# Local attention in 20 chunks of 116 or 112 queries instead of 24 of 96, with q and k of a chunk in one load

## The chip, the cores and the metric

The kernel runs on one core of a Trainium2 chip. The metric is the device time of one execution in microseconds (us). A core has a matrix engine (PE, with its weight loads shown apart as PEld), a vector engine (DVE), an activation engine (ACT), a general engine (POOL), and a queue engine (SP) that here only issues DMAs. Each engine works through its own instructions in the order in which the program issues them.

## What is computed

Three stages in float32. B, H, S, D are 4, 8, 576, 64, so there are 2304 tokens of 512 values.

```python
# local + downsampled attention (S = 576, factor = 4)
q_d, k_d, v_d = (x.reshape(B, H, S // 4, 4, D).mean(axis=3) for x in (q, k, v))
out_up = np.repeat(sm_attn(q_d, k_d, v_d), 4, axis=2)
mask = np.abs(pos[:, None] - pos[None, :]) < 4
scores = np.where(mask, scale * q @ k.T, -1e9)
attn = np.exp(scores - max); attn = attn / (sum + 1e-09)
x = (out_up + attn @ v).reshape(B * S, H * D)
# MoE1, then MoE2, 512 -> 2048 -> 512 on each token
h = x @ w_in;  x = (h * sigmoid(h)) @ w_out
h = x @ w_in2; out = (P(h) / (Q(h) + 1e-6)) @ w_out2
```

The weights and activations of the two MoE stages are each split into a high and a low part, and a product takes three matmuls (high by high, low by high, high by low).

## The kernel before, in words

**Attention** is made batch by batch (`attention(b)`, line 375). For each batch three loads bring k and q (line 392, 192 queries each). The downsampled attention takes sums of four (line 408 for batch 0, accumulating DMAs at lines 435 and 437 for the others) and runs through lines 471 to 526. The local attention of a batch is cut into 6 chunks of 96 queries, each two halves of 48 that lie on partitions 0 and 64. A chunk is a chain of jobs:

- S, lines 569 to 583, on PE: two matmuls of 216 columns that put the band mask into PSUM, and 16 small matmuls of 64 rows and 54 keys. The trace records each small float32 matmul twice, so S has 2 + 32 records.
- M (587), E (593 and 597, eight exponentials), U (602 and 603, sum and reciprocal), N (606, normalizing).
- T, line 617, on PE: eight transposes of 48 queries; C (line 627, the copy function at 332 or 328) brings them to SBUF.
- O, line 637, on PE: 16 small matmuls of 48 columns with v (32 records).
- A (644) adds the downsampled part, H (655) and X (659) split the result into `xh` and `xl`.

**MoE1** runs over 5 blocks of tokens: four of 5 chunks (480 columns) and one of 4 chunks (384 columns). A block takes 16 steps, one for each 128 rows of the hidden layer. A step has 12 matmuls at line 807 (h) and, two steps later, 12 at line 821 (o); all have as many columns as the block. Blocks 0 and 1 are interleaved: 8 steps of block 0, 16 of block 1, 8 of block 0, then blocks 2 to 4 (`PART1`, line 311). Step 0 needs all chunks of block 0, step 8 all of block 1.

**The weights** arrive as float64 and are converted on the chip, 64 pieces with seven jobs each on DVE, ACT and POOL (`piece`, line 699). MoE1's pieces must be ready for steps 0 to 7 (w_in, w_out of f = 0 to 7) and 16 more for steps 16 to 23. MoE2's are converted while MoE1 runs.

**The order of the work** on every engine until the end of MoE1 is set when the program is built: a planner (`Plan.run`, line 122) simulates the jobs with assumed costs, due times, and rings of buffers, and emits them in the order of its simulation. In the first part it also puts matmuls that compute nothing (line 289, 256 columns) where it expects PE to idle. MoE2 (from line 1041) follows in a written order, 5 blocks of 512 or 384 tokens.

Of the kernel before, what the change touches and what calls it, by code (L numbers as in the profile page):

```python
# [10 lines left out]
F32 = mybir.dt.float32  # L11
# [10 lines left out]
CH = 96  # L22
SUB = 48
HALO = 3
WK = SUB + 2 * HALO
TH = 2 * CH
KW = TH + 2 * HALO
QPAD = 16
BLOCKS1 = [5, 5, 5, 5, 4]
# [18 lines left out]
NKQ = 4  # L48
# [200 lines left out]
def r_ns(n, count):  # L249

    return count * (n / 2.4 + 14)
# [3 lines left out]
def tile_kernel(ctx, tc, kq, kqs, vp, vw_in, moe_w_in, moe_w_out, moe2_w_in, moe2_w_out, moe2_a, moe2_b, out):  # L255
# [10 lines left out]
    NCH = S // CH  # L266
    NB1 = max(BLOCKS1) * CH

# [36 lines left out]
    chunk_block = [(j, i) for j, n in enumerate(BLOCKS1) for i in range(n)]  # L305
    tok0, t = [], 0
    for n in BLOCKS1:
        tok0.append(t)
        t += n * CH

# [5 lines left out]
    for j, f in STEP1:  # L316
        guess.append(t)
        t += 24 * (BLOCKS1[j] * CH / 2.4 + 14) * PACE
# [23 lines left out]
    E_t = [at.tile([128, 8, 64], F32, tag=f"E{i}", name=f"E{i}", bufs=1) for i in range(NE)]  # L342
# [18 lines left out]
    nc.vector.memset(bands[64:128, 2, :, WK - HALO:WK], NEG)  # L361
    for e in E_t:
        nc.gpsimd.memset(e[:, :, WK:], 0.0)
        nc.gpsimd.memset(e[:, :, WK:WK + 1], 1e-9)
# [10 lines left out]
    def attention(b):  # L375
# [6 lines left out]
        def tail(b, c):  # L382
            j, i = chunk_block[b * NCH + c]
            return when[j * NF] - LEAD + 300.0 * i


        loads = []
        for t in range(3):
            u = kqu[t] = Unit("kq")
            def ld(e, t=t):  # L390
                kqt[t] = at.tile([128, KT * (KW + TH) + QPAD], F32, tag="kq", name="kq", bufs=NKQ)
                nc.sync.dma_start(out=kqt[t], in_=kq[b, t])
            loads.append(plan.add(f"L{b}{t}", FAR, {"D": 60}, ld, take=[u],
                                  size=128 * 4 * 1576))
# [3 lines left out]
        if b == 0:  # L398
            for t in range(3):
                for w in range(2):  # L400
                    def sm(e, t=t, w=w):
                        if w == 0:
                            o = kd[:, :, SUB * t:SUB * t + SUB]
                            i = kqt[t][:, :KT * KW].rearrange("p (g s) -> p g s", g=KT)[:, :, HALO:HALO + TH]
                        else:
                            o = qd[:, :KT * SD].rearrange("p (g s) -> p g s", g=KT)[:, :, SUB * t:SUB * t + SUB]
                            i = kqt[t][:, KT * KW:KT * (KW + TH)].rearrange("p (g s) -> p g s", g=KT)
                        nc.vector.tensor_reduce(out=o, in_=i.rearrange("p g (j r) -> p g j r", r=4), axis=AX.X, op=ALU.add)
                    sums.append(plan.add(f"R{b}{t}{w}", FAR, {"V": v_ns(768)}, sm, after=[loads[t]] + sums[:1],
                                         take=[] if sums else [kdu], give=[kqu[t]]))  # L410
# [49 lines left out]
        for m in range(2):  # L460
# [4 lines left out]
            def s(e, x=x, m=m, p0=p0):  # L465
                x["s"] = pair(p0)
                for t in range(3):
                    for a in range(2):
                        for e_ in range(2):
                            r, g = slice(64 * e_, 64 * e_ + 64), 2 * m + a  # L470
                            nc.tensor.matmul(x["s"][64 * a:64 * a + 64, e_, SD * t:SD * t + SD],  # L471
                                             lhsT=qd[r, SD * g + SUB * t:SD * g + SUB * t + 64], rhs=kd[r, g, :],
# [26 lines left out]
            def tr(e, x=x, e_=0, u=None):  # L499
                x["t", e_] = pair(u)  # L500
                for t in range(3):
                    for kk in range(2):
                        for a in range(2):
                            r = slice(64 * a, 64 * a + SUB)
                            nc.tensor.transpose(x["t", e_][:HS, a, SD * kk + SUB * t:SD * kk + SUB * t + SUB],
                                                x["e"][r, 3 * e_ + t, HS * kk:HS * kk + HS], ident[r, r])
# [39 lines left out]
        for c in range(NCH):  # L546
            x = {}
            j, i = chunk_block[b * NCH + c]
            due = begin[j] - (TAIL1 if j == 1 else TAIL) - (STAG if j else STAG0) * (BLOCKS1[j] - 1 - i)
            t, q0 = c // 2, CH * (c % 2)  # L550
# [18 lines left out]
            def s(e, x=x, c=c, t=t, q0=q0, pS=pS):  # L569
# [5 lines left out]
                for g in range(KT):  # L575
                    for s_ in range(2):
                        for e_ in range(2):
                            r = slice(64 * e_, 64 * e_ + 64)
                            k0 = KW * g + q0 + SUB * s_
                            l0 = KT * KW + TH * g + q0 + SUB * s_  # L580
                            nc.tensor.matmul(sp[64 * s_:64 * s_ + 64, e_, WK * g:WK * g + WK],  # L581
                                             lhsT=kqt[t][r, l0:l0 + 64], rhs=kqt[t][r, k0:k0 + WK],
# [8 lines left out]
            def ex(e, x=x, eu=eu):  # L591
                x["e"] = E_t[eu.no]
                nc.scalar.activation(x["n"], x["n"], AF.Copy, scale=D ** -0.5)
                for e_ in range(2):
                    for g in range(KT):
                        i = KT * e_ + g
                        nc.scalar.activation(x["e"][:, i, :WK], x["s"][:, e_, WK * g:WK * g + WK], AF.Exp,  # L597
                                             scale=D ** -0.5, bias=x["n"][:, i:i + 1])

            def su(e, x=x):  # L600
                x["r"] = at.tile([128, 8], F32, tag="r1", name="r1", bufs=4)
                nc.vector.tensor_reduce(out=x["r"], in_=x["e"][:, :, :WK + 1], axis=AX.X, op=ALU.add)
                nc.vector.reciprocal(out=x["r"], in_=x["r"])

            def no(e, x=x):
                eng(e).tensor_tensor(out=x["e"][:, :, :WK], in0=x["e"][:, :, :WK],
                                     in1=x["r"].unsqueeze(2).to_broadcast([128, 8, WK]), op=ALU.mult)

            def tr(e, x=x, pT=pT):

                tp = x["t"] = pair(pT)
                for e_ in range(2):
                    for m in range(2):
                        for s_ in range(2):
                            r = slice(64 * s_, 64 * s_ + SUB)
                            i, o = KT * e_ + 2 * m, SUB * (2 * e_ + m)
                            nc.tensor.transpose(tp[:, s_, o:o + SUB],  # L617
                                                x["e"][r, i:i + 2].rearrange("q a k -> q (a k)"), ident[r, r])

            def cp_(e, x=x, c=c):  # L620
# [6 lines left out]
                copy(e, x["p"], x["t"][:, :, :4 * SUB])  # L627

            def pv(e, x=x, pO=pO):
                op = x["o"] = pair(pO)  # L630
                for m in range(2):
                    for s_ in range(2):
                        for e_ in range(2):
                            for a in range(2):
                                r = slice(64 * a, 64 * a + WK)
                                o = SUB * (2 * e_ + m)
                                nc.tensor.matmul(op[64 * e_:64 * e_ + 64, a, CH * m + SUB * s_:CH * m + SUB * s_ + SUB],  # L637
                                                 lhsT=x["v"][r, s_, 2 * m + e_, :], rhs=x["p"][r, s_, o:o + SUB],
                                                 start=True, stop=True)

            def ad(e, x=x, c=c):
# [542 lines left out]
```

## Time and profile before

| | before |
|---|---|
| median of 3 runs (lowest to highest) | 926.54 us (924.27 to 926.77) |
| span of the profiled execution | 923.6 us |
| mean granted clock of TensorE | 0.996 |
| busy: PE, DVE, ACT, POOL | 906.2, 711.4, 606.8, 333.2 us |
| start of step 0 of MoE1 / of step 8 (its block 1) | 46.9 / 112.2 us |
| start of the last O / of the first matmul of MoE2 | 418.5 / 518.8 us |

The profiled execution's own time is the 923.6 us of its span, from its first to its last instruction; the median of the runs is 2.9 us above that. Busy time of PE is modelled from pipelined matmuls, so the distance from the start of one matmul to the start of the next, not the time of one, tells what a matmul costs in a stream.

### The profile page before, as it was taken

The numbers are of one execution on the slowest core, as the hardware profiler recorded it, in microseconds if no ns is written. First come the engines' busy times: TensorE is split into PE (matmuls) and PEld (weight loads), VectorE is DVE, ScalarE is ACT, GpSimd is POOL, SyncE is SP. The second block draws the span as 40 slices with busy tenths as digits, with TensorE's granted clock in tenths as the row PEclk, the third lists the DMA queues.
The fourth block names the chain that finished last, engine by engine and source line by source line (L and its number), as shares of the span: only waits on it lengthen the run. The fifth ranks groups of instructions, "written<-read, shape, count | busy, mean of one in ns | idle before, by whom it ended". The sixth has DMA issues, their size and how long they took to land.

```text
span 923.6 us, 16216 instructions
## 1 busy us (share of the span) xinstructions
PE 906.2 (98%) x6212; PEld 762.3 (83%) x6212; DVE 711.4 (77%) x1060; ACT 606.8 (66%) x1224; POOL 333.2 (36%) x279
## 2 busy tenths in 40 slices
PE   8988999999999999999999999999999999999997
PEld 6766788877887778878899988888888888999996
DVE  6979876996557876785332399998998999799995
ACT  4957655786446764674322488877877777787874
POOL 4534240142022410121000155655555555455553
PEclk9989999999999999999999999999999999999999
DMA  9878997779789777779685091002001000200000
GB/s 282 287 217 247 277 282 279 251 268 301 220 269 294 238 276 276 268 245 363 213 288 210 5 392 48 1 1 92 1 1 48 33 1 1 80 1 0 35 1 35
DMA packets 48042, 153.03 MB, mean 166 GB/s; under 512 B 5244, under 2 KB 10492, under 8 KB 47964
## 3 DMA queue, kind: packets, MB, share of 16 engines
q1 hardware_dynamic: 44972, 143.03, 44.1%
q0 software_dynamic: 2704, 8.95, 5.4%
q8 instruction: 49, 0.80, 0.4%
q14 instruction: 29, 0.24, 0.1%
q10 hardware_dynamic: 288, 0.00, 0.0%
HBM read 116.38 MB, written 35.59 MB: 165 GB/s over the span
## 4 chain that ended last, share of the span: by engine, by line
PE 91%; DVE 4%; ACT 3%; issue 1%; POOL 0%; ACTq 0%; DVEq 0%; POOLq 0%
PE hps L807 43%; PE acc L1054 21%; PE acc L821 21%; PE wps L289 1%; PE pair L637 1%; PE pair L581 1%; PE pair L519 1%; ACT E L597 1%; PE pair L617 1%; DVE cw L735 1%; ACT cr L723 0%; DVE cr L732 0%; ACT PT L332 0%; DVE cw L728 0%; PE pair L471 0%
## 5 line engine op out<-in xcount | busy, mean ns | idle before, releaser
L807 PE MATMUL hps<-xh,w 128*128 128x480 f32 (+1 forms) x640 | 226.0, 381 | 3.6 <-DVE th L973 3.0
L821 PE MATMUL acc<-gh,wo 128*128 128x480 f32 (+1 forms) x640 | 222.8, 376 | 0.0
L807 PE MATMUL hps<-x2h,wi 128*128 128x512 f32 (+1 forms) x640 | 196.4, 368 | 0.0
L894 POOL TENSOR_TENSOR u<-u,ah 128x512 f32<-128x512 f32 (+1 forms) x80 | 96.0, 1200 | 262.7 <-ACT u L892 261.1
L1054 PE MATMUL acc<-wo,gh 128*128 128x512 f32 x576 | 178.0, 390 | 0.0
L807 PEld LDWEIGHTS hps<-xh,w 128*128 128x128 f32 x640 | 121.1, 189 | 22.5 <-DVE th L973 3.8
L821 PEld LDWEIGHTS acc<-gh,wo 128*128 128x128 f32 x640 | 119.8, 188 | 17.4 <-issue 1.8
L807 PEld LDWEIGHTS hps<-x2h,wi 128*128 128x128 f32 x640 | 118.8, 188 | 16.3
L1085 POOL TENSOR_TENSOR gl<-p,gh 128x512 fp32r<-128x512 f32 (+1 forms) x80 | 121.2, 1515 | 11.6 <-issue 8.9
L1054 PEld LDWEIGHTS acc<-wo,gh 128*128 128x128 f32 x576 | 107.6, 188 | 20.9
L807 PE MATMUL hps<-xl,w 128*128 128x480 f32 (+1 forms) x320 | 120.0, 375 | 1.1 <-DVE xl L659 1.0
L821 PE MATMUL acc<-gl,wo 128*128 128x480 f32 (+1 forms) x320 | 118.6, 371 | 0.4 <-POOL gl L982 0.4
L807 PE MATMUL hps<-x2l,wi 128*128 128x512 f32 (+1 forms) x320 | 117.7, 368 | 0.0
L1054 PE MATMUL acc<-wo,gl 128*128 128x512 f32 x288 | 112.7, 391 | 0.0
L970 ACT ACTIVATE th<-hps 128x480 f32<-128x480 f32 (+1 forms) x80 | 44.5, 557 | 101.7 <-PE hps L807 100.8
L973 DVE SCALAR_TENSOR_TENSOR th<-th,hps 128x480 f32<-128x480 f32 (+1 forms) x80 | 50.4, 631 | 78.9 <-ACT th L970 78.5
L1077 DVE SCALAR_TENSOR_TENSOR u<-u,r 128x512 f32<-128x512 f32 (+1 forms) x80 | 100.1, 1252 | 2.8
L1070 ACT ACTIVATE r<-u,cst 128x512 f32<-128x512 f32 (+1 forms) x80 | 54.5, 682 | 52.7 <-POOL u L894 52.7
L1076 DVE SCALAR_TENSOR_TENSOR u<-u,r 128x512 f32<-128x512 f32 (+1 forms) x80 | 82.7, 1034 | 0.5 <-ACT r L1071 0.5
L732 POOL TENSOR_TENSOR cr<-cw,cr 128x512 int32<-128x512 int32 x22 | 30.9, 1407 | 135.0 <-DVE cw L728 86.2
L891 DVE TENSOR_TENSOR p<-p,hps 128x512 f32<-128x512 f32 (+1 forms) x80 | 50.5, 631 | 31.5 <-ACT p L890 31.3
L332 ACT ACTIVATE gh<-th 128x480 fp32r<-128x480 f32 (+1 forms) x80 | 47.4, 592 | 31.8 <-DVE th L973 28.5
(123 smaller groups left out, 1485.4 us busy)
## 6 DMA issues: line engine op xcount, KB each, us to landing
wo<-wos SPq DMA_DIRECT2D x64, 512.0 KB, 5.8
raw<-moe_w_in SPq DMA_DIRECT2D x32, 512.0 KB, 5.0
raw<-moe_w_out SPq DMA_DIRECT2D x32, 512.0 KB, 5.9
w2s<-cvo SPq DMA_DIRECT2D x32, 512.0 KB, 5.2
kq<-kq SPq DMA_DIRECT2D x12, 788.0 KB, 7.5
wos<-wo SPq DMA_DIRECT2D x16, 512.0 KB, 3.1
wi<-w2s SPq DMA_DIRECT2D x16, 512.0 KB, 6.6
wo<-w2s SPq DMA_DIRECT2D x16, 512.0 KB, 9.7
```

The source lines that it names most:

```text
L332: nc.scalar.activation(out, in_, AF.Copy, scale=scale)
L807: nc.tensor.matmul(hps[:, :n], lhsT=wi[:, i, 128 * g:128 * g + 128], rhs=(a, b)[s][:, g, :n], start=(m == 0), stop=(m == len(mms) - 1))
L821: nc.tensor.matmul(acc_t[p][g // 2][:, g % 2, :n], lhsT=wo[:, i, 128 * g:128 * g + 128], rhs=s_[:, :n], start=(f == f0 and m % 3 == 0), st ...
L891: nc.vector.tensor_tensor(out=p, in0=p, in1=hps, op=ALU.mult)
L894: nc.gpsimd.tensor_tensor(out=u, in0=u, in1=ah, op=ALU.mult)
L970: nc.scalar.activation(x["t"][:, :n], x["h"][:, :n], AF.Tanh, scale=0.5)
L973: nc.vector.scalar_tensor_tensor(out=x["t"][:, :n], in0=x["t"][:, :n], scalar=1.0, in1=x["h"][:, :n], op0=ALU.add, op1=ALU.mult)
L1054: nc.tensor.matmul(acc2[j][c], lhsT=a[:, 128 * c:128 * c + 128], rhs=wo[:, i, :], start=(f == 0 and m % 3 == 0), stop=(f == NF - 1 and m % ...
L1070: nc.scalar.activation(r, u, AF.Ln, scale=2.0 ** -64, bias=cst[:, 0:1])
L1076: nc.vector.scalar_tensor_tensor(out=u, in0=u, scalar=1.000001, in1=r, op0=ALU.add, op1=ALU.mult)
L1077: nc.vector.scalar_tensor_tensor(out=u, in0=u, scalar=-2.0, in1=r, op0=ALU.add, op1=ALU.mult)
L1085: nc.gpsimd.tensor_tensor(out=gl2[k_][:, :n], in0=p, in1=gh2[k_][:, :n], op=ALU.subtract)
```

## The change

The batch's 576 queries are cut into chunks of 116, 116, 116, 116 and 112 (halves of 58 and 56), so there are 5 chunks for each batch and 20 in all. A half sees 64 keys instead of 54, which fills the rows of the tiles that had been padded to 64. k and q of one chunk come in one load of 496 KB (five for each batch, in 6 buffers) instead of 788 KB for two chunks (three for each batch, in 4 buffers). The sum over the row in U loses its padding column of 1e-9, and a DVE instruction on 128x8 values adds 1e-9 instead. A block of MoE1 is 4 chunks: one block of 464 columns and four of 460, 2304 in all as before. The downsampled attention keeps its pieces of 48. Some cost figures of the planner change too. MoE2 and the weight conversion are not touched.

```diff
-CH = 96
-SUB = 48
+CHUNKS = [116, 116, 116, 116, 112]
+CH = max(CHUNKS)
+SUB = CH // 2
 HALO = 3
 WK = SUB + 2 * HALO
-TH = 2 * CH
-KW = TH + 2 * HALO
+KW = CH + 2 * HALO
+TS = 48
-BLOCKS1 = [5, 5, 5, 5, 4]
+NB = 4
...
-NKQ = 4
+NKQ = 6
...
-    return count * (n / 2.4 + 14)
+    return count * (n / 2.4 + 17)
...
+    sizes = CHUNKS * B
+    BLOCKS1 = [sum(sizes[i:i + NB]) for i in range(0, len(sizes), NB)]
+    NB1 = max(BLOCKS1)
...
-        for t in range(3):
+        for t in range(NCH):
             u = kqu[t] = Unit("kq")
             def ld(e, t=t):
-                kqt[t] = at.tile([128, KT * (KW + TH) + QPAD], F32, tag="kq", name="kq", bufs=NKQ)
+                kqt[t] = at.tile([128, 2 * KT * KW + QPAD], F32, tag="kq", name="kq", bufs=NKQ)
                 nc.sync.dma_start(out=kqt[t], in_=kq[b, t])
...
-            for t in range(3):
-                for w in range(2):
...
+            for t in range(NCH):
+                def sm(e, t=t):
+                    o = kqd[:, :2 * KT * SD].rearrange("p (g s) -> p g s", g=2 * KT)[:, :, at0[t] // 4:(at0[t] + CHUNKS[t]) // 4]
+                    i = kqt[t][:, :2 * KT * KW].rearrange("p (g s) -> p g s", g=2 * KT)[:, :, HALO:HALO + CHUNKS[t]]
+                    nc.vector.tensor_reduce(out=o, in_=i.rearrange("p g (j r) -> p g j r", r=4), axis=AX.X, op=ALU.add)
...
-                            k0 = KW * g + q0 + SUB * s_
-                            l0 = KT * KW + TH * g + q0 + SUB * s_
+                            k0 = KW * g + sub * s_
+                            l0 = KW * (KT + g) + HALO + sub * s_
                             nc.tensor.matmul(sp[64 * s_:64 * s_ + 64, e_, WK * g:WK * g + WK],
-                                             lhsT=kqt[t][r, l0:l0 + 64], rhs=kqt[t][r, k0:k0 + WK],
+                                             lhsT=kqt[c][r, l0:l0 + 64], rhs=kqt[c][r, k0:k0 + WK],
...
-                nc.vector.tensor_reduce(out=x["r"], in_=x["e"][:, :, :WK + 1], axis=AX.X, op=ALU.add)
+                nc.vector.tensor_reduce(out=x["r"], in_=x["e"], axis=AX.X, op=ALU.add)
+                nc.vector.tensor_scalar(out=x["r"], in0=x["r"], scalar1=1e-9, scalar2=None, op0=ALU.add)
                 nc.vector.reciprocal(out=x["r"], in_=x["r"])
...
-                            r = slice(64 * s_, 64 * s_ + SUB)
-                            i, o = KT * e_ + 2 * m, SUB * (2 * e_ + m)
-                            nc.tensor.transpose(tp[:, s_, o:o + SUB],
+                            r = slice(64 * s_, 64 * s_ + sub)
+                            i, o = KT * e_ + 2 * m, sub * (2 * e_ + m)
+                            nc.tensor.transpose(tp[:, s_, o:o + sub],
...
-            js = plan.add(f"S{b}{c}", d0, {"P": 900}, s, after=[loads[t]], take=[pS, eu], give=[kqu[t]],
+            js = plan.add(f"S{b}{c}", d0, {"P": 1000}, s, after=[loads[c]], take=[pS, eu], give=[kqu[c]],
...
-        n = BLOCKS1[j] * CH
+        n = BLOCKS1[j]
```

## Rows read from the trace of the kernel before

**Rows 1.** The page's part 1: busy time, share of the span, instructions of each engine.

```profile
PE 906.2 (98%) x6212; PEld 762.3 (83%) x6212; DVE 711.4 (77%) x1060; ACT 606.8 (66%) x1224; POOL 333.2 (36%) x279
```

**Rows 2.** PE, PEld, DVE, ACT, POOL busy us (and counts) by stage, granted clock, DMA share, GB/s.

```profile
0.00:46.90 46.90, 41.99 (x844) 32.82 (x845) 37.26 (x78) 32.61 (x114) 24.85 (x40) 1.00 0.90 284
54.00:112.20 58.20, 54.96 (x501) 41.79 (x501) 48.74 (x86) 39.52 (x88) 20.10 (x18) 0.95 0.81 239
112.20:380.00 267.80, 267.69 (x2078) 218.15 (x2079) 196.90 (x346) 163.48 (x365) 61.71 (x51) 1.00 0.82 266
```

**Rows 3.** Chain that ended last, 45 to 130 us: start us, us, what.

```profile
54.01 5.17 PE hps L807 x12
...
112.19 0.55 DVE xl L659
...
112.78 3.96 PE hps L807 x17
```

**Rows 4.** Timeline of PE, steps 60 to 63 and 69 to 79: start us, us, line.

```profile
428.32 0.38 PE L807 MATMUL hps<-xh,w 128*128 128x480 f32 x1
...
443.96 0.38 PE L807 MATMUL hps<-xh,w 128*128 128x480 f32 x1
...
470.39 0.34 PE L807 MATMUL hps<-xh,w 128*128 128x384 f32 x1
...
512.52 0.34 PE L807 MATMUL hps<-xh,w 128*128 128x384 f32 x1
```

**Rows 5.** Timeline of PE, an O, a T and an S between MoE1's matmuls.

```profile
402.53 0.38 PE L821 MATMUL acc<-gh,wo 128*128 128x480 f32 x1
402.85 0.68 PE L637 MATMUL pair<-PT,vw 54*64 54x48 f32 x32
403.46 0.48 PE L807 MATMUL hps<-xh,w 128*128 128x480 f32 x1
403.78 0.38 PE L807 MATMUL hps<-xl,w 128*128 128x480 f32 x1
...
404.64 0.38 PE L821 MATMUL acc<-gh,wo 128*128 128x480 f32 x1
...
405.66 0.38 PE L807 MATMUL hps<-xl,w 128*128 128x480 f32 x1
405.87 0.37 PE L807 MATMUL hps<-xh,w 128*128 128x480 f32 x1
406.09 0.36 PE L572 MATMUL pair<-bands,ident 128*128 128x216 bf16 x2
406.38 0.69 PE L581 MATMUL pair<-kq 64*64 64x54 f32 x32
406.99 0.49 PE L807 MATMUL hps<-xh,w 128*128 128x480 f32 x1
407.32 0.38 PE L807 MATMUL hps<-xl,w 128*128 128x480 f32 x1
```

**Rows 6.** Timeline of PE: small matmuls of 144 columns, and what follows them.

```profile
183.54 0.97 PE L471 MATMUL pair<-kqd 64*64 64x144 f32 x24
184.43 0.48 PE L821 MATMUL acc<-gh,wo 128*128 128x480 f32 x1
```

**Rows 7.** Groups by line and shape, ACT and DVE: count, busy us, mean ns of one.

```profile
L597 ACT ACTIVATE E<-pair,n 128x54 f32<-128x54 f32 x152 | 31.9, 322 | 0.8
L973 DVE SCALAR_TENSOR_TENSOR th<-th,hps 128x480 f32<-128x480 f32 x64 | 41.5, 650 | 41.4 <-ACT th L970 41.1
L973 DVE SCALAR_TENSOR_TENSOR th<-th,hps 128x384 f32<-128x384 f32 x16 | 8.9, 554 | 37.5 <-ACT th L970 37.5
```

**Rows 8.** DMA issues by line in the first 20 us: KB, median us to landing.

```profile
kq<-kq SPq DMA_DIRECT2D x3, 788.0 KB, 6.7
```

**Rows 9.** Waits of PE and of the queue engine: us in total, times, longest.

```profile
PE hps L807 <- DVE th L973: 3.0, 1, 3.0
...
SPq L782 <- POOL wo L743: 40.4, 7, 11.9
```

## What is predicted

> **What bounds the kernel now.** I read the busy times first: PE works 906.2 of 923.6 us, the next engine 711 [rows 1]. A share over the whole span hides stages, so I read the stages next [rows 2]. From 112.2 us on PE has no idle time worth the name (267.69 of 267.80 us), while DVE has 197 and ACT 163 in the same stretch: there, what PE is spared shortens the kernel, and nothing else does. Before that it is not so plain. Up to 46.9 us PE is busy 42.0 us, but part of this is the empty matmuls of line 289, and the DMA engines are at 0.90, DVE at 37.3. From 54 to 112.2 us PE has 55.0 of 58.2 us and DVE 48.7, with 0.95 of the clock. The chain [rows 3] then shows what ends this stretch: step 8 of MoE1 goes on at 112.78 when DVE has written the last `xl` of block 1, at 112.74. So the kernel is: a mixed part until block 1's chunks are all in, then PE alone until the end.
>
> **Prices on PE.** From step 60 to step 63 there is no attention between the matmuls: (443.96 - 428.32) us over 72 matmuls of 480 columns is 217.2 ns each. Steps 69 to 79 give (512.52 - 470.39) over 240 matmuls of 384, 175.5 ns [rows 4]. For a chunk I take the distance between MoE1's matmuls with a piece between them, less two matmuls of 217 ns [rows 5]: O 403.78 - 402.53 - 0.434 = 0.816 us, T 405.66 - 404.64 - 0.434 = 0.586, S 407.32 - 405.87 - 0.434 = 1.016. A chunk costs 2.42 us of PE. These are three places; the other pieces in the full stretch look the same.
>
> **Part 1: small matmuls in the full stretch.** Blocks 0 and 1 take 10 of 24 chunks before and 8 of 20 after, so 14 chunks stand behind step 8 before and 12 after. What one of the 12 costs no row shows at 58 or 64 columns. In S the two mask matmuls go from 216 to 256 columns: the nearest slope is that of the large matmuls, 41.7 ns for 96 columns [rows 4], hence 80 columns x 0.434 = +0.035 us. For the float32 ones: 32 records of 54 columns take 406.99 - 406.38 = 0.61 us, 32 records of 48 columns in O take 403.46 - 402.85 = 0.61 too [rows 5]. So six columns cost nothing, 19 ns a record either way. At 144 columns 24 records take 184.43 - 183.54 = 0.89 us, 37 ns a record [rows 6]. The line from 54 to 144 is 0.2 ns a column, for S's ten columns +0.064 us. The lower end is zero; the upper end is in proportion to columns, +0.11 (S), +0.13 (O) and, on T's 0.38 us, +0.08. I take +0.064 for S and nothing for O and T, because 58 columns lie next to the flat pair of 48 and 54: 2.42 + 0.035 + 0.064 = 2.52 us (2.45 to 2.78). Then 14 x 2.42 = 33.9 becomes 12 x 2.52 = 30.2: **-3.6 us** (-4.5 to -0.5).
>
> The Trainium skill, in "TensorE: Matmul & The Clock Gate", section "Back-to-back issue gap", puts 1 to 64 columns at one and the same 60 cycles. By it, S and O don't grow, the chunk is 2.45 us and the part -4.5 us; the two rows at 0.61 us agree up to 54 columns, and none goes to 64.
>
> **Part 2: MoE1's matmuls.** Their number stays 1920 and their columns stay 2304 a pass; only the split moves. On the line between 175.5 ns (384) and 217.2 ns (480), 464 columns cost 210.2 and 460 cost 208.5 ns. Behind step 8 there are 72 steps of 24. Before: 56 x 24 x 217.2 + 16 x 24 x 175.5 = 359.3 us. After: 8 x 24 x 210.2 + 64 x 24 x 208.5 = 360.6: **+1.3 us**, since a shorter first block hands columns to the later ones. The bounds: columns at 1/2.4 ns with the surplus of 384 (15.5 ns) or of 480 (17.2 ns) on top, -0.9 to +2.0 us. The first eight steps get shorter by 8 x 24 x 7.0 ns = 1.3 us; this belongs to the next part.
>
> **Part 3: until step 8.** Two chunks fewer must be through (464 + 460 = 924 tokens instead of 960). On PE that is 10 x 2.42 - 8 x 2.52 = 4.0 us and the 1.3 us above: 5.3 us if PE alone bounded the stretch. On ACT a chunk's eight exponentials take 31.9 us / 19 chunks = 1.68 us; eighty more elements add about 0.08 at the 1.0 ns that 96 elements cost on DVE (650 - 554 ns) [rows 7], so 10 x 1.68 against 8 x 1.76 is 2.7 us less. DVE makes about five passes a chunk of some 0.6 us (an instruction of 384 elements is 0.554): 10 x 3.0 against 8 x (3.0 + 5 x 0.08 + 0.1 for the added instruction) is 2.0 us less. The stretch is shared, so I take **-3.0 us**, between the 2.0 of DVE and the 5.3 of PE and nearer to DVE, whose `xl` ends it. Hidden: a batch's loads grow from 3 x 788 KB to 5 x 496 KB, 0.12 MB or 0.4 us at 284 GB/s, ahead of the last sum of batch 0; three of the four batches load long before use. Fewer `vw` loads take 1.05 MB off the queue in all. Two more load issues stand on SP ahead of the weights' loads of each batch, well under a microsecond.
>
> **The sum**, against the profiled 923.6 us: -3.6 + 1.3 - 3.0 = -5.3, so a span of 918.3. The median of the runs lies 2.9 us above the span; carried along, the forecast is **921.2 us**, 0.6% less. With the bounds that are likely together its own range is 918.2 to 924.2.
>
> **Rivals.** (a) *The new order loses its hole.* The order before has one: step 1 waits 3.0 us for DVE [rows 9], and PE, having idled, then runs step 1 at 5.17 us for 12 matmuls [rows 3], 431 ns each, half of the granted clock, 2.6 us more than twelve at 217. Each engine's order is made anew; without this hole 5.6 us more are gained: 915.6. (b) *It gets a second one.* SP issues in order and was held once for 11.9 us by a store that waited for POOL [rows 9]; another such hold in the first 112 us starves the conversion and costs another 5.6: 926.8. Nothing in the trace says which, but (a) has one thing to lose and (b) needs a new one. (c) *Small matmuls grow in proportion*: 12 x (2.78 - 2.52) = +3.1, 924.3. The flat pair speaks against it.
>
> (d) *Loads go one by one.* The first loads of 788 KB land 6.7 us after issue [rows 8], while 284 GB/s [rows 2] would need 2.8; if the other 3.9 were paid for each of the five in turn, two more would put batch 0's last sum 7.8 us later: 929.0. Against it: DMA engines are at 0.90 there, so transfers already run beside one another. The Trainium skill, in "DMA: Bandwidth & Descriptors", section "Anatomy of one DMA", gives about 2.0 us fixed for each DMA issued from GpSimd, and advises fewer, larger ones; by that, two more in a row would cost 4.0 us and the sum would be 925.2. It speaks against the change, and no row here shows a row of loads that don't overlap.
>
> (e) *Slower: 460 columns cost more than the line says.* Every count of MoE1 and MoE2 in the trace is a multiple of 128 or is 480. If 464 and 460 were paid as the next multiple of 32, that is 480, the price is 384 x 7.0 ns + 1536 x 8.7 ns = 16.1 us: 937.3. It cancels the gain at 2.8 ns a matmul (5.3 us / 1920) and makes the kernel measurably slower at 4.2 ns. 384 and 480 lie on one line with a surplus of 15.5 and 17.2 ns, which doesn't suggest steps, but can't exclude them, since both are multiples of 32.
>
> **How the numbers follow.** A measurement of this kernel tells some 0.3%, 2.8 us, from no change: faster means under 923.8, slower over 929.3. Forecast 0.50 (0.45 faster, 0.05 same); (a) 0.17, faster; (b) 0.15 (0.13 same, 0.02 slower); (c) 0.07 (0.02 faster, 0.05 same); (d) 0.05 (0.03 same, 0.02 slower); (e) 0.06, slower. Together faster 0.64, same 0.26, slower 0.10. The range goes from 914.5, under (a), to 927.5, over (b) and (c); left out are (d), (e) and the tails of (a) and (b), about 0.2.
>
> **What the profile of the changed kernel would show.** Part 1: 20 pieces each of S, T and O instead of 24, and S at about 1.11 us, O and T unchanged, between MoE1's matmuls. Part 2: 208 to 209 ns from start to start in steps without attention; 217 would be (e). Part 3: step 8 starting near 109 us instead of 112.2; a start before 105 is (a), after 115 is (b), and the waits of PE and SP in the first 112 us name it. (d) would show in batch 0's five loads landing one after another, some 4 us apart. The forecast is wrong if PE is found idle in the stretch behind step 8, which none of its steps allows for.

## The result, and the profile after

The changed kernel takes 932.3 us (median; 931.81 to 932.72) beside 926.18 us for the kernel before (924.27 to 926.77) on the same chip: ratio 1.0073, interval 1.0056 to 1.009. It is slower by 0.7%, where 0.6% faster was forecast. The profiled executions have spans of 930.9 and 923.6 us, so 7.3 us are to be found.

The page's part 1 of the kernel after; the columns are those of [rows 1]:

```profile
PE 903.4 (97%) x5917; PEld 760.9 (82%) x5917; DVE 721.3 (77%) x1054; ACT 598.9 (64%) x1179; POOL 334.0 (36%) x271
```

PE has less to do than in [rows 1], as forecast, and DVE more. The view of windows, first of the kernel before and then of the one after, from the start of step 8 to the start of MoE2 (columns as in [rows 2]):

```profile
112.20:518.80 406.60, 406.49 (x3008) 343.89 (x3009) 262.82 (x464) 221.38 (x494) 71.83 (x59) 1.00 0.78 260
```

```profile
107.10:519.90 412.80, 407.21 (x2871) 348.52 (x2870) 270.55 (x465) 215.52 (x472) 79.94 (x64) 1.00 0.78 257
```

In this stretch PE was never idle before (0.1 of 406.6 us) and is idle for 5.6 us after. For each stage I also price PE's work: MoE1's matmuls at 217.2, 175.5, 210.2 and 208.5 ns for 480, 384, 464 and 460 columns, the attention pieces at their medians between MoE1's matmuls. What is left of a stage is "other time": waits, matmuls at a lower clock, and pieces that run longer. All in us, worked out from PE's start times in the one profiled execution of each kernel:

| | before | after |
|---|---|---|
| start of step 8 | 112.2 | 107.1 |
| step 8 to MoE2, MoE1's matmuls | 357.7 | 360.0 |
| step 8 to MoE2, attention pieces | 48.0 | 44.0 |
| step 8 to MoE2, other time | 1.0 | 8.8 |
| MoE2, first eight steps | 34.2 | 37.5 |
| MoE2, the other steps, to the start of the last | 350.8 | 354.1 |
| from MoE2's last step to the end | 19.7 | 19.4 |

The differences are -5.1, +2.3, -4.0, +7.8, +3.3, +3.3 and -0.3, together +7.3 us. The steps that were costed brought 6.8 us; 7.8 us went to other time behind step 8, of which 5.5 is more idle time of PE, and 6.6 us to MoE2 from its first step to its last, which the diff doesn't touch.

PE's longest waits in the kernel after, from 107 to 520 us (total us, times, longest):

```profile
PE pair L607 <- ACT EE L476: 1.9, 1, 1.9
PE acc L810 <- ACT w L333: 1.4, 1, 1.4
```

The chain of the kernel after, from 160 to 206 us (start us, us, what):

```profile
159.86 1.89 PE hps L796 x9
...
185.96 1.66 DVE cw L706
...
191.77 0.60 DVE r L591
...
192.40 0.18 DVE r L592
...
193.37 0.60 DVE E L596
193.97 0.56 DVE th L962
194.57 2.51 PE hps L796 x6
```

For over 30 us, from 161.75 to 194.57, the chain runs through DVE, ACT and POOL, which convert weights (`cw`) and do softmax in between; PE only follows. "Then PE alone until the end" no longer holds here. When PE comes back, six matmuls take 2.51 us, 418 ns each. The windows view of the stretch before, of these six, and of the stretch behind them (the granted clock is the third figure from the end):

```profile
188.00:194.50 6.50, 4.41 (x46) 3.20 (x44) 6.40 (x12) 3.25 (x10) 1.36 (x2) 1.00 0.95 346
194.50:197.10 2.60, 2.53 (x7) 1.80 (x8) 2.57 (x5) 1.88 (x4) 1.16 (x1) 0.56 0.41 165
197.10:204.00 6.90, 6.87 (x74) 5.57 (x76) 5.04 (x10) 3.96 (x13) 2.14 (x2) 0.92 0.71 191
```

PE was busy for 4.41 of 6.50 us and then got 0.56 of its clock, near the lower level of 1.2 GHz; the 1.9 us of waiting cost another 1.25 us (6 x 209 ns). It is the same pairing as in [rows 3], a wait and then matmuls at half the clock, at a new place.

### The profile page after: what moved, and what is told of

Same layout as the page of the kernel before. It is cut to its first block, busy times and chain, and to the rows that moved or that the text cites. A ratio compares the mean times of both kernels' runs of the same rounds, so it can differ in the third digit from the quotient of the medians.

```text
span 930.9 us, 15532 instructions
## 1 busy us (share of the span) xinstructions
PE 903.4 (97%) x5917; PEld 760.9 (82%) x5917; DVE 721.3 (77%) x1054; ACT 598.9 (64%) x1179; POOL 334.0 (36%) x271
## 4 chain that ended last, share of the span: by engine, by line
PE 76%; DVE 5%; issue 2%; ACT 2%; DMA 1%; POOL 1%; SPq 0%; ACTq 0%; POOLq 0%; DVEq 0%
PE hps L796 36%; PE acc L1043 21%; PE acc L810 16%; DVE cr L721 1%; DVE cw L715 1%; PE pair L627 1%; DVE cw L724 1%; DMA x2s<-xe 1%; DMA wo<-wos 1%; PE pair L508 0%; DVE cw L717 0%; PE pair L570 0%; DVE r L591 0%; PE pair L607 0%; POOL cvo L732 0%
## 5 line engine op out<-in xcount | busy, mean ns | idle before, releaser
L796 PE MATMUL hps<-xh,w 128*128 128x460 f32 (+1 forms) x640 | 220.4, 378 | 4.5 <-DVE th L962 1.9
L810 PE MATMUL acc<-gh,wo 128*128 128x460 f32 (+1 forms) x640 | 220.4, 377 | 1.4 <-ACT w L333 1.4
L796 PE MATMUL hps<-xl,w 128*128 128x460 f32 (+1 forms) x320 | 119.3, 373 | 0.5 <-DVE xl L648 0.5
L810 PE MATMUL acc<-gl,wo 128*128 128x460 f32 (+1 forms) x320 | 118.5, 370 | 0.0
L962 DVE SCALAR_TENSOR_TENSOR th<-th,hps 128x460 f32<-128x460 f32 (+1 forms) x80 | 50.2, 628 | 83.8 <-ACT th L959 83.6
L959 ACT ACTIVATE th<-hps 128x460 f32<-128x460 f32 (+1 forms) x80 | 44.7, 559 | 106.4 <-PE hps L796 105.6
L971 DVE TENSOR_TENSOR gl<-th,gh 128x460 fp32r<-128x460 f32 (+1 forms) x77 | 53.3, 692 | 27.5 <-ACT gh L333 27.0
L333 ACT ACTIVATE gh<-th 128x460 fp32r<-128x460 f32 (+1 forms) x80 | 47.0, 587 | 39.6 <-DVE th L962 29.0
## 6 DMA issues: line engine op xcount, KB each, us to landing
wi<-w2s SPq DMA_DIRECT2D x16, 512.0 KB, 10.1
```

The lines of the kernel that those rows point to most:

```text
L333: nc.scalar.activation(out, in_, AF.Copy, scale=scale)
L796: nc.tensor.matmul(hps[:, :n], lhsT=wi[:, i, 128 * g:128 * g + 128], rhs=(a, b)[s][:, g, :n], start=(m == 0), stop=(m == len(mms) - 1))
L810: nc.tensor.matmul(acc_t[p][g // 2][:, g % 2, :n], lhsT=wo[:, i, 128 * g:128 * g + 128], rhs=s_[:, :n], start=(f == f0 and m % 3 == 0), st ...
L962: nc.vector.scalar_tensor_tensor(out=x["t"][:, :n], in0=x["t"][:, :n], scalar=1.0, in1=x["h"][:, :n], op0=ALU.add, op1=ALU.mult)
L971: eng(e).tensor_tensor(out=gl_t[s][:, :n], in0=x["t"][:, :n], in1=gh_t[s][:, :n], op=ALU.subtract)
```

## The experiments

Two theories stood at the start: *addresses* (the larger `bands` moves every tile behind it, and MoE2's matmuls pay) and *order* (the change also raises the durations by which the planner places PE's work, so that the engines' order is another). The rivals were DVE as an engine at its limit behind step 8, and the loads. A third theory came from the first results: the one small instruction that the change adds to DVE, `tensor_scalar` by 1e-9 on line 592.

**Addresses.** `bands` grows by 224 bytes a partition, rounded to 32, and all tiles behind it move. In the kernel after, 32 more bytes are left free, which restores the remainders; in the kernel before 224, or 64, are added, which spoil them.

```
after_pad32      +    cp.tile([128, 16], BF16, name="gap")     # behind bands
before_pad224    +    cp.tile([128, 112], BF16, name="gap")
before_pad64     +    cp.tile([128, 32], BF16, name="gap")
```

> The changed kernel with 32 bytes a partition left free behind the mask tile; the computation and the order are the same. In the changed kernel the mask tile grew from 1296 to 1536 bytes and moved every tile on the left side of SBUF by 224 bytes, so they start at 0 modulo 64 while the tiles of the right side start at 32 modulo 64; before, all start at 32 modulo 64, and with the 32 bytes they do so again. Theory (a matmul with its weights and its moving data on different remainders is slower): in MoE2 the steps of 233 to 234 ns a matmul return to 227, MoE2 gets 4 to 6 us shorter, the median is 926 to 929 us. Rival (MoE2 is slow because of what POOL, DVE or DMA do there): MoE2 stays at about 392 us from its first to its last h step, the median at 932.

> The kernel before with 224 bytes a partition left free behind the mask tile, so that in MoE2 every tile lies where it lies in the changed kernel. Nothing else differs. Theory of the remainders: MoE2 shows 233 to 234 ns in the same steps as the changed kernel and gets 4 to 6 us longer, the median is 930 to 932 us; MoE1, whose tiles all lie on the left side and move together, stays the same. Rival: no change, 926.

> The kernel before with 64 bytes left free behind the bands: nothing else changes. Left-hand tiles go from remainder 96 to 32 modulo 128, and keep 32 modulo 64; right-hand ones stay. Theory A (what counts is whether weights and moving data lie on the same remainder modulo 64): MoE2's matmuls all stay at 227 ns, time as before, within 1 us. Theory B (modulo 128): 233 ns in the same blocks as with 224 bytes, MoE2 some 3.5 us longer, ratio near 1.0036.

Measured: 928.65 us (1.0032, 1.0018 to 1.0046), 3.7 us less than the kernel after; 929.44 (1.0036, 1.0023 to 1.0049); 929.07 (1.0034, 1.0023 to 1.0044). PE's timeline in one step of MoE2, its first and twelfth matmul, in the kernel before and then in the one after:

```profile
553.06 0.39 PE L807 MATMUL hps<-x2h,wi 128*128 128x512 f32 x1
...
555.55 0.39 PE L807 MATMUL hps<-x2h,wi 128*128 128x512 f32 x1
```

```profile
557.36 0.40 PE L796 MATMUL hps<-x2h,wi 128*128 128x512 f32 x1
...
559.93 0.39 PE L796 MATMUL hps<-x2h,wi 128*128 128x512 f32 x1
```

Eleven matmuls in 2.49 us are 226 ns each, in 2.57 us 234 ns, with no wait between them. With the 32 bytes such steps are back at 226 to 227 ns, and from MoE2's first step to its last 391.6 us become 388.1; with 224 or 64 bytes in the kernel before, 385.0 become 388.9 and 388.2. By the program's allocation (a profile shows no addresses) left-hand tiles lie at 96 modulo 128 in the kernel before and with 32 bytes, at 64 in the one after and with 224, at 32 with 64 bytes; right-hand ones stay at 96. So 32 modulo 64 alone isn't enough. Whether weights and moving data must agree modulo 128 or modulo 256 is open: a shift by 128 was not tried.

That it is the pair, and not the place of the left-hand tiles, can be read from the blocks. MoE2's weights of f = 0 to 3 lie on the right and the others on the left; its moving data lie on the right in blocks 0 and 2 and on the left in block 1 (all of 512 columns). In the kernel after, the steps of blocks 0 and 2 with left-hand weights take 233 to 234 ns a matmul; in block 1 those with right-hand weights take 233, and those with both on the left stay at 227 to 230. The blocks of 384 columns pay nothing (174 to 177 ns, 176 before). This cause is shown in both directions: 3 to 4 us.

**The loads alone.** The kernel before with its 24 chunks of 96, but one load of q and k for each chunk:

```
-NKQ = 4
+NKQ = 8
...
-        for t in range(3):
+        for t in range(NCH):
...
-  kqt[t] = at.tile([128, KT * (KW + TH) + QPAD], ...)
+  kqt[t] = at.tile([128, 2 * KT * KW + QPAD], ...)
...
```

> One part alone: the kernel before, 24 chunks of 96, but k and q of each chunk in a load of its own (six loads of 416 KB for each batch in 8 buffers instead of three of 788 KB in 4, and one sum over q and k for each chunk of batch 0). Rival of the prediction (loads go one by one, each with its fixed time): batch 0's sums end 4 us or more later, median 928 to 930. Theory (loads run beside one another): the sums end within 1 us of where they did, 925 to 928, what remains being the order.

Measured: 921.84 us (0.9959, 0.9945 to 0.9972). Step 8 starts at 108.8 us, and other time behind it is 0.5 us. This half of the change, with the order that the planner makes for it, is a gain of 0.4%, more than expected. How much of it is the loads and how much that order isn't shown.

**The planner's figures.** PE's planned time of one of MoE1's matmuls (n / 2.4 + 14 ns before, + 17 after), and of S, T and O (900, 500, 700 before, 1000, 530, 770 after), put back in the kernel after, and put into the kernel before:

```
after_oldcosts     -    return count * (n / 2.4 + 17)
                   +    return count * (n / 2.4 + 14)
                   S {"P": 1000} -> 900, T 530 -> 500, O 770 -> 700
before_newcosts    the reverse
after_both         after_oldcosts with the gap of 32 bytes
```

> The changed kernel with the planner's four cost figures of the kernel before for PE: matmul surplus 14 ns instead of 17, S 900 instead of 1000, T 500 instead of 530, O 700 instead of 770. Theory (the raised figures took away slack: with the low ones the planner believes PE faster than it is, so DVE and ACT run ahead of PE's order by more and more, with the raised ones PE arrives at a piece before its producer): PE's waits of 0.6 to 1.9 us at 122, 183, 194 and 394 us go, and MoE1 gets 4 to 6 us shorter, median 926 to 929. Rival (DVE and ACT bound the stretch whatever the order): the waits stay in sum, at other places, median 930 to 934.

> The kernel before with the changed kernel's four cost figures for PE (17 ns, 1000, 530, 770). Theory of the lost slack: PE gets waits of about a microsecond each in MoE1 where it had none, 2 to 6 us in all, median 928 to 932. Rival (the figures don't matter, the chunks do): 925 to 928.

> The changed kernel with both: 32 bytes free behind the mask tile and the four old cost figures in the planner. If the two causes are separate, their gains add: 932.3 - 3.7 - 4.2 = 924.4 us, some 1.5 to 2 below the kernel before (925.9 on this chip's last runs). If they are two faces of one thing, 927 to 929.

Measured: 928.14 us (1.0032, 1.002 to 1.0044), 930.35 (1.0051, 1.0036 to 1.0066), 923.74 (0.9982, 0.9972 to 0.9991). The figures move the time by 4 to 5 us each time, and address and figures add up: with both put back the change is 0.2% faster than the kernel before. But the idle time doesn't go as I thought: other time behind step 8 is 7.6 us with the old figures in the kernel after (8.8 with the new ones), while in the kernel before the new ones bring it from 1.0 to 5.3.

**DVE's load.** In MoE2's 32 weight conversions DVE's clamp is left out (that part of the output differs), in the version of 923.74 us and, as a control, in the kernel before; and the planner gets longer DVE and POOL figures for softmax.

```
after_both_noclamp, before_noclamp
+            if "2." not in name:
                 nc.vector.tensor_scalar(out=x["w"], in0=x["w"], scalar1=W_LOW, scalar2=W_HIGH, ...)
after_both_dvecosts
 M {"V": v_ns(8 * WK)} + 70; U + 270 -> + 500; N "V" + 90, "G" 130 -> 420
```

> As after_both, without the clamping instruction in the conversion of MoE2's 32 weight pieces (the first DVE instruction of c3, 0.4 us each; weights out of the float32 range come out different). The planner's costs are unchanged, so every engine has the same order; DVE has some 13 us less to do in MoE1. Theory (PE's waits in MoE1 come from pieces whose producers on DVE are late): of PE's 5 to 6 us of waits behind step 8 at least 3 us go, and the median is 3 us or more below after_both. Rival (the waits are of the order itself, on buffers or DMA): less than 1 us.

> The control: the kernel before without the same instruction. Behind step 8 PE has no waits to lose there (0.7 us in all), so theory and rival both expect little there; before step 8, where DVE ends the stretch, few of these pieces are made. Under 1.5 us in all, 924.5 to 926.5.

> As after_both, with the add, but the planner is told what the trace shows for the wide chunks' jobs: U 230 ns more, M 70 more, N 90 more on DVE and 290 more on POOL. The work is the same, the order changes. Theory (PE comes before its producers because the plan believes them faster than they are): PE's waits behind step 8 fall from 7.0 to under 4 us, median 920 to 923. Rival (DVE and ACT are the bound there whatever the plan says): 923 to 926.

Measured: 921.42 us (0.996, 0.9948 to 0.9973), 925.33 (0.9993, 0.9983 to 1.0003), 923.73 (0.9985, 0.9976 to 0.9994). Less DVE work gives 2.3 us where DVE makes PE wait and nothing that can be measured where it doesn't, but less than the 3 us that I expected. The longer figures bring other time behind step 8 from 7.0 to 2.2 us, and step 8 starts 4.5 us later: nothing gained. This plan shifted the wait, it didn't remove it.

**The added instruction.** The groups of line 592 and its neighbour, in the kernel after and then in the version of 923.74 us (count, busy us, mean ns):

```profile
L592 DVE TENSOR_SCALAR r<-r 128x8 f32<-128x8 f32 x20 | 7.6, 382 | 0.7
L593 DVE RECIPROCAL r<-r 128x8 f32<-128x8 f32 x20 | 4.1, 203 | 0.7
```

```profile
L593 DVE TENSOR_SCALAR r<-r 128x8 f32<-128x8 f32 x20 | 12.1, 604 | 0.7
```

Eight elements a partition take 382 or 604 ns, while the reciprocal of the same shape takes 203 in both. The timeline of the kernel after shows why (DVE and POOL, 392 us):

```profile
391.48 0.69 DVE L591 TENSOR_REDUCE r<-E 128x8 f32<-128x512 f32 x1 [0.19 <-ACT E L586]
392.09 1.30 POOL L732 TENSOR_TENSOR cvo<-cw,cvo 128x512 fp32r<-128x512 f32 x1 [5.77 <-ACT cvo L333]
392.20 1.22 DVE L592 TENSOR_SCALAR r<-r 128x8 f32<-128x8 f32 x1
393.45 0.20 DVE L593 RECIPROCAL r<-r 128x8 f32<-128x8 f32 x1
```

POOL's instruction started at 392.09 and ends at 393.39; the add, started within it, ends at 393.42. Of the 20, fifteen take 0.17 us; the five longer ones (0.49 to 1.27 us) each started while POOL worked and end 27 to 30 ns after that instruction of POOL. The Trainium skill, "SBUF — State Buffer", section "SBUF: two separate sides", says that DVE and GpSimd share a pair of ports, that certain DVE instructions and GpSimd's exclude one another on it, and that whoever comes second is blocked for the other's whole instruction. The trace agrees for the add (0.17 to 1.27 us), and the reciprocals (202 to 206 ns) are not held up: in the version without the add, below, one that starts 0.43 us into an instruction of POOL takes 204 ns. So the instruction was taken out (the output changes by less than its rounding; the order of all other instructions stays), and put into the kernel with the new loads alone:

```
after_both_noadd
-                nc.vector.tensor_scalar(out=x["r"], in0=x["r"], scalar1=1e-9, scalar2=None, op0=ALU.add)
loads_alone_add  the same line added; U {"V": v_ns(440) + 200} -> + 270
```

> As after_both, without the DVE instruction that adds 1e-9 to the 128x8 sums (a sum holds exp(0) = 1, so in float32 the value is the same). The planner's costs and so every engine's order are unchanged. In after_both's trace these 20 instructions take 604 ns each, 12.1 us in all, while the reciprocal on the same shape takes 203 ns; the long ones stand while POOL works. Theory (this instruction makes the producers late): PE's time behind step 8 that is neither a MoE1 matmul nor a piece of attention falls from 7.0 us to 4 or less, median 1.5 to 4 us below after_both (923.7), that is 920 to 922. Rival (the wait moves to the next DVE instruction, which needs the same access): under 0.7 us.

> The kernel with 24 chunks of 96 and one load for each chunk, with the same adding instruction put into U (24 times, 1e-9 once more, no change of the value in float32) and 70 ns for it in the planner, as in the change. Theory (the instruction is what costs): PE's waits behind step 8 rise from 0.5 us to 2 to 5, median 923 to 926 instead of 921.8. Rival (it costs its 0.2 us on an engine with room): within 1 us of 921.8.

Measured: **916.69 us** (0.991, 0.9896 to 0.9925), 7.0 us less than with it, and faster than both kernels; 931.3 us (1.0061, 1.0047 to 1.0075), 9.5 us more than without. Both go beyond what was expected. In the second, the planner's figure for U grew too and made another order: step 8 starts at 114.2 us instead of 108.8, other time behind it is 3.0 instead of 0.5, and before step 8 the granted clock is 0.94 on average instead of 0.98. In the first, where the order stays, other time goes from 7.0 to 4.8 us and step 8 starts 1.7 us earlier (profiled executions of 923.6 and 919.6 us). I took the instruction for the main cause then. Is it also worth that in the kernel after, with its own figures?

```
after_noadd         the kernel after without that line
after_pad32_noadd   the same, with the gap of 32 bytes
```

> The changed kernel without DVE's add of 1e-9 to the sums (the output differs by less than its rounding), the same order of all other instructions, the planner's new figures and the old addresses kept. Theory (the added instruction, held up behind POOL's, makes the waits of PE behind step 8 and delays DVE before it): as in the pair of kernels with old figures and 32 bytes of gap, where it was worth 7.0 us, so 932.3 - 7 = 925 us (923 to 927), other time of PE behind step 8 down from 8.8 to 5 to 6 us, step 8 a good 1 us earlier than 107.1. Rival (the planner's new figures make an order without slack, whatever DVE does): under 3 us gained, 929.5 or more, other time still above 7 us.

> The same with 32 bytes left free behind the bands, which puts MoE2's operands back on the remainders of the kernel before. Theory (three causes that add up: the added instruction 7, the addresses 3.7, the planner's figures 4 us): 928.65 - 7 = 921.6 us (920 to 923.5), and the distance to the same kernel with the old figures, 916.69, is the 4 to 5 us that the figures cost. Rival (the figures cost something only because of the added instruction): 917 to 919.

Measured: 930.93 us (1.0054, 1.0038 to 1.0071) and 926.81 (1.0004, 0.999 to 1.0019). No: 1.4 and 1.8 us, and in both pairs the intervals of the two ratios overlap, so neither is clear of noise. Other time behind step 8 stays at 8.9 and 8.1 us: the wait that ends at 194 us had the add at only 0.18 us in its chain (192.40). What the traces, one execution of each kernel, show of the add lies before step 8, which starts at 103.7 instead of 107.1 us, and with the gap at 103.9 instead of 110.1. The rival held, that the planner's figures make an order that waits whatever DVE does. All eight but one of the combinations are now there (medians, us; the kernel before took 925.5 to 926.2 beside them):

| | no gap | gap of 32 |
|---|---|---|
| new figures, add | 932.3 | 928.65 |
| old figures, add | 928.14 | 923.74 |
| new figures, no add | 930.93 | 926.81 |
| old figures, no add | not run | 916.69 |

The gap is worth 3.7, 4.4 and 4.1 us, whatever else there is. The old figures are worth 4.2, 4.9 and 10.1, the missing add 1.4, 1.8 and 7.0: these two depend on each other, or rather the add's price depends on the order.

**Which figure, and is it a direction?** From the version of 916.69 us, one input of the planner at a time:

```
noadd_step17   n / 2.4 + 14 -> + 17
noadd_step14   S, T, O 900, 500, 700 -> 1000, 530, 770
noadd_step11   n / 2.4 + 14 -> + 11
after_both_noadd_margin   MARGIN 800 -> 1600
```

> The changed kernel with 32 bytes of gap and without the add, planned with 17 ns of surplus for each of MoE1's matmuls (as in the change) and the old 900, 500 and 700 ns for S, T and O. With all new figures this kernel took 926.8 us, with all old ones 916.7. Theory (the 3 ns for each of 1920 matmuls, 5.8 us of planned time, spread the rest of the plan so that DVE's and ACT's work is placed later): most of the 10 us stays, 924 to 928 us, with the wait for ACT's copy at about 119 us and other time of PE behind step 8 near 8. Rival (the figures of the pieces do it): 916 to 919, other time below 5.

> The other half: 14 ns of surplus, and the change's 1000, 530 and 770 ns for S, T and O. Theory (the matmuls' figure does it): 916 to 919 us, other time of PE behind step 8 below 5. Rival (the pieces' figures do it): 924 to 928, and near 8.

> As the version of 916.7 us, with 11 ns of surplus in place of 14. Theory (a plan that thinks PE faster than it is puts the others' work earlier, which is slack): 913 to 917 us, other time of PE behind step 8 at 4 or less. Rival (each set of figures gives another order, and its time is chance within some 5 us): anything, 920 us or more as likely as not; also a start of step 8 that moves by more than 3 us from 105.5.

> As after_both_noadd, with the planner's margin ahead of PE's pieces of batches 1 to 3 raised from 800 to 1600 ns, so that PE comes to a piece later than its producers are planned to end. Theory of late producers: what is left of PE's waits behind step 8 falls by half or more, median 0.5 to 2 us below after_both_noadd. Rival (the order's other ends move, step 8 above all, which the plan puts later): step 8 starts later by what is saved, median the same or 1 to 3 us above.

Measured: 930.7 us (1.006, 1.0037 to 1.0083), 920.89 (0.9945, 0.9923 to 0.9966), 924.85 (1.0001, 0.9986 to 1.0016) and 930.96 (1.0053, 1.0039 to 1.0067). The matmuls' figure alone costs 14 us upwards (17 ns) and 8 us downwards (11 ns), the pieces' figures 4 us, and matmuls' and pieces' together only 10. So it is no direction in which slack grows; that theory falls. Three of the four times lie outside what theory and rival had given; only the rival of `noadd_step11`, that each set of figures gives another order and its time is chance, held. The same instructions, in orders planned from six sets of inputs (these four, 916.69 and 926.81), take from 916.7 to 931.0 us. The loss lies at other places each time. The chain of the kernel planned with 17 ns:

```profile
232.26 1.75 ACT E L587 x8
...
234.05 0.59 PE pair L562 x2
```

PE waits 3.24 us here for a chunk's softmax, because PE's order has a second S there ahead of MoE1's next matmul; other time behind step 8 is 10.9 us. The wait isn't the whole price. After 0.88 and 1.18 us of idle time PE has the lower clock from 230.0 us on (windows view):

```profile
230.00:240.20 10.20, 6.96 (x78) 5.73 (x74) 7.38 (x14) 4.41 (x20) 1.04 (x1) 0.50 0.99 270
```

It is busy for 6.96 of these 10.2 us at 0.50 of its clock; half of that, some 3.5 us, is my estimate of what the clock adds to the waits. With 11 ns other time is 5.1 us and step 8 starts at 104.4, but MoE2's first eight steps take 41.4 us (35.0 with 14 ns), with two waits there (total us, times, longest):

```profile
PE acc L1043 <- POOL gl L1074: 1.8, 1, 1.8
PE acc L1043 <- ACT gh L1073: 1.3, 1, 1.3
```

There too the clock is at 0.50, for 6.8 us from 536.1 us on.

With the pieces' figures (920.89) other time is 1.5 us and step 8 starts at 109.7 instead of 105.5.

## Why the prediction was wrong, point by point

**Part 1, the small matmuls (-3.6): right.** PE's timeline of the kernel after, an S and a T between matmuls of 460 columns:

```profile
281.61 0.37 PE L796 MATMUL hps<-xh,w 128*128 128x460 f32 x1
281.82 0.39 PE L561 MATMUL pair<-bands,ident 128*128 128x256 bf16 x2
282.15 0.69 PE L570 MATMUL pair<-kq 64*64 64x64 f32 x32
282.77 0.48 PE L810 MATMUL acc<-gh,wo 128*128 128x460 f32 x1
283.09 0.37 PE L810 MATMUL acc<-gl,wo 128*128 128x460 f32 x1
...
286.43 0.37 PE L810 MATMUL acc<-gh,wo 128*128 128x460 f32 x1
286.72 0.46 PE L607 MATMUL pair<-ident,E 58*128 58x58 f32 x8
287.11 0.47 PE L810 MATMUL acc<-gh,wo 128*128 128x460 f32 x1
287.42 0.37 PE L810 MATMUL acc<-gl,wo 128*128 128x460 f32 x1
```

S: 283.09 - 281.61 - 2 x 0.209 = 1.06 us; T: 0.57. The medians are 1.06, 0.59 and 0.82 us (S, T, O), a chunk 2.47 where 2.52 was taken; 32 records of 64 columns take 282.77 - 282.15 = 0.62 us, as those of 48 and 54 in [rows 5]. The flat pair goes on to 64 columns. Rival (c) is refuted.

**Part 2, the matmuls of MoE1 (+1.3): right in price.** The first matmuls of steps 64 and 79:

```profile
438.42 0.37 PE L796 MATMUL hps<-xh,w 128*128 128x460 f32 x1
...
513.63 0.37 PE L796 MATMUL hps<-xh,w 128*128 128x460 f32 x1
```

(513.63 - 438.42) over 15 steps of 24 is 208.9 ns, where the line of [rows 4] gave 208.5. 460 columns aren't paid as 480 [rows 4]: rival (e) is refuted. That the stretch has 2.3 us more of them and not 1.3 comes from where step 8's start falls among the other matmuls: with the old figures in the plan it is 1.9 us less.

**Part 3, until step 8 (-3.0): the sign came out, its size and its reason are open.** The profile after has -5.1. But the version with the gap, whose order is the same, starts step 8 at 110.1 us, -2.1. The windows view of the kernel after and then of that version:

```profile
0.00:107.10 107.10, 91.71 (x1201) 70.68 (x1201) 93.71 (x171) 73.45 (x193) 40.07 (x47) 1.00 0.86 262
0.00:110.10 110.10, 95.82 (x1201) 73.16 (x1201) 94.61 (x171) 73.79 (x193) 40.78 (x47) 0.95 0.83 255
```

The granted clock is 1.00 in the one and 0.95 in the other; in the kernel before it is 0.97 up to step 8, with the hole of rival (a) in it. So that hole's matmuls at half the clock are missing from the execution that gave -5.1, and its size isn't that of the chunks alone. The new loads, which the part had as a small cost, start step 8 at 108.8 without any chunk fewer. The right sign is luck in part.

Batch 0's sums, in the profile before and then in the one after (durations, first and last start):

```profile
L408 DVE TENSOR_REDUCE kqd<-kq x6: 942/943/954, 6.7 to 15.9; 128x192 f32<-128x768 f32 x6
L397 DVE TENSOR_REDUCE kqd<-kq x5: 1069/1110/1123, 5.8 to 16.5; 128x232 f32<-128x928 f32 x4, 128x224 f32<-128x896 f32 x1
```

The five start 2.7 us apart on average, and the last one 0.6 us later than the last of the six before, where rival (d) gave 7.8; (d) is refuted. A term of this part that was mis-sized is the added instruction: "0.1" us a chunk was taken, and it took 0.38 on average and up to 1.27. That works against the gain, so it doesn't explain the -5.1.

**The step that failed is "then PE alone until the end"**, read from [rows 2]. It was read from one order of the engines and held for all. The forecast named its own refutation, PE idle behind step 8, and that is what happened: 5.6 us of idle time where there was 0.1, and 7.8 us more other time. Rival (b) had the right kind of thing, another hole of the order, but only in the first 112 us and at 5.6 us. In [rows 2] DVE has 197 and ACT 163 of 268 us busy, enough room on average. A full DVE isn't the explanation by itself; from 160 to 194 us, before and then after:

```profile
160.00:194.00 34.00, 34.00 (x224) 28.03 (x223) 32.65 (x55) 25.94 (x59) 7.02 (x5) 1.00 0.70 245
160.00:194.00 34.00, 31.47 (x249) 26.42 (x249) 31.02 (x52) 23.32 (x61) 14.11 (x10) 1.00 0.81 283
```

DVE is busy for 32.65 us before, and PE never waits; it is busy for 31.02 us after, and PE is idle for 2.5. What remains is the order of the work, which is argued from this and from the runs with other plans.

The second thing missing is MoE2, which I held to be untouched and gave no term in the sum: +6.6 us, of which the gap gives back 3.5. Of the rest, 1.6 is a wait of PE for POOL's `gl` in its first steps,

```profile
PE acc L1043 <- POOL gl L1074: 1.6, 1, 1.6
```

which the runs with old figures don't have (35.0 us for eight steps with old figures and gap, 37.5 after), and 0.8 are two of MoE1's last matmul groups that now have 460 columns instead of 384; 0.7 us stay unexplained.

So what turned a gain into +0.7% is the addresses, +3.7 us, and the order, in which the planner's new figures cost 4.2 us and which the six plans show to be worth up to 14; with these two put back the change takes 923.74 us, 0.2% less than the kernel before. The instruction is worth 1.4 us in the order of the kernel after, which isn't clear of noise. Without it, with the gap and the old figures, it is 916.69 us, 9 us less than the kernel before; but that is the best of six orders (the next is 920.89), and the kernel before was tried in one other order only (930.35). What the change is worth apart from its order isn't shown. Why one plan waits and another doesn't was followed in single places only; that the waits change place with the plan is shown, a rule for it isn't.

## What to carry to other kernels

A share of busy time, and a stretch without idle time too, belongs to one order of the engines: when a change makes a planner work anew, give the order a term of its own with both signs, as wide as plans from slightly altered inputs scatter (here 1.5%). Before trusting a comparison, try the change's parts with the old inputs of the plan, and keep the addresses of large operands on the remainders they had. A small DVE instruction of a kind that POOL can hold up, here `tensor_scalar`, is to be priced up to POOL's longest instruction beside it, not by its elements. A wait of PE is to be priced with the matmuls behind it, where the trace shows them at half the clock.

## What the runs showed of the hardware

- In MoE2's h steps (line 807 before, 796 after) of 512 columns, TensorE's matmuls take 226 to 230 ns from start to start in the kernel before, where weights and moving data all lie on the same remainder modulo 128 bytes, and 233 to 234 ns in 28 of the 48 steps after, the 28 with weights and moving data on different remainders; 64 bytes of shift do it as well as 224, but in block 1 those steps then take 229 ns, and steps of 384 columns take 173 to 177 ns either way. What tells these apart was not tried.
- A DVE `tensor_scalar` of 8 elements a partition takes 0.17 us alone and up to 1.27 us when it starts within POOL's `tensor_tensor`, and ends 27 to 30 ns after it; reduction (644 to 689 ns) and reciprocal (202 to 206 ns) next to it keep their times.
- Some waits of PE are followed by stretches at the lower level of its clock: 1.9 us of idle time by 0.56 of the clock over 2.6 us in the kernel after, 0.88 and 1.18 us by 0.50 over 10.2 us with 17 ns.
- float32 matmuls of 48, 54 and 64 columns take the same 19 ns a record.
